# Two v loads issued from GpSimd's DMA queue instead of SyncE's, in a linear-attention and MLP kernel

## The chip, the cores and the metric

The kernel runs on one core of a Trainium2 chip. The metric is the device time of one execution in microseconds (us), as the median of several runs; the profiled execution is a further one, read by the hardware profiler.

A core has five engines that run side by side, each through its own list of instructions in order: TensorE (PE, with the weight loads as PEld), VectorE (DVE), ScalarE (ACT), GpSimd (POOL) and SyncE (SP). They wait for one another by semaphores. Loads from memory are DMAs, which an engine's queue issues and which the core's 16 DMA engines carry out.

## The reference

The first part is a gated linear attention with a state per head, over 4 batches, 8 heads, 768 positions and head size 48. The second is an MLP with the gate h * cos(h) on the 3072 tokens that result, each with 8 * 48 = 384 values.

```python
f = 1.0 / (1.0 + np.exp(-f_logit))
state = np.zeros((B, H, D, D))
for t in range(S):
    state = f[:, :, t, :, None] * state + np.einsum('bhd,bhe->bhde', k[:, :, t], v[:, :, t])
    y[:, :, t] = np.einsum('bhd,bhde->bhe', q[:, :, t], state)
x = y.transpose(0, 2, 1, 3).reshape(B * S, H * D)
h = x @ w_in                  # 384 -> 2048
out = (h * np.cos(h)) @ w_out # 2048 -> 384
```

## The kernel before

**Tiles.** The positions of a batch are taken 256 at a time; such a stretch, for all 8 heads, is a "pair" n, two neighbouring positions on each of the 128 partitions; there are 12 pairs, three for each batch. For a pair the kernel loads f, k, q and v, each as a tile of 128 partitions x 8 heads x 96 values in float32, 384 KB. Each head's 96 values on a partition are one contiguous run of 384 bytes in memory, so such a load has 1024 of these runs. For pairs 0 and 1 the loads of f, k and q are cut in two by heads (names f0.0, f0.1 and so on); v is not. The tiles come from pools of three buffers for each kind.

**Steps of a pair.** On ACT the logarithm of the gate is made from f (ex, ln, fx); TensorE sums it up along the positions (cum), ACT turns the sums into the decays eb and ei; qa and ka finish the factors of q and k, qm and km multiply them with the decays and write bf16 into the tile qk. For pairs 0 and 1, qm and km are given to POOL or VectorE one by one. TensorE turns q and k (tq, tk, line 435), VectorE or ACT copies the result from PSUM (qkt, line 197), TensorE makes the scores (sc, line 456), VectorE masks them (am, line 461). v is cast to bf16 in the tile vb (step vb, line 197), for pairs 0 and 1 by ACT, and four copies bring it in another order into vt. TensorE makes the state's increments from vb and qk (ps, line 479), VectorE carries the state (st, sz, lines 497 and 503), and TensorE makes the outputs (y, yi, line 531). The casts xe bring them to the MLP as x.

**The MLP.** It runs in units of 128 or 256 tokens: h (line 579) on TensorE, the cosine (co, line 584) on ACT, the product (g, line 561) on VectorE, and o (line 595) on TensorE. Its weights w0 and w1 are loaded and cast once (steps w and wc), beside the first pairs.

**Order.** The text ORDER writes out by hand, step by step, which engine does what, and in which order: the letter behind the colon is the engine (T TensorE, S ACT, V VectorE, G POOL, Y SyncE), the digits are buffer numbers. Each engine gets its steps in this order and does not overtake; a step waits on semaphores for what it reads and for the buffer that it writes. All loads stand on SyncE, except one half of f0 on ACT. Steps zf (line 264) are matmuls of zeros at the beginning that fill TensorE's time while there is no other work; their results aren't used.

The steps around the change, in the order of their engines: SyncE issues f0.1, k0.0, k0.1, f1.1, f1.0, q0.1, q0.0, then v0, f3, k1.1, k1.0, v1, f2, q1.0, q1.1, w0.1, w0.0. POOL has km0.0, qm0.0, a memset, ka1.0, ka1.1, km1.1. ACT has eb0.0, vb0, eb1.0, vt0.3, ei1.0, ex3 (of pair 3), eb1.1, ln3, ei1.1, vt0.0, vb1, ex2 (of pair 2). TensorE has ps0.1, ps0.0, tk0.1, tq0.0 after a group of zero matmuls.

The loads are issued by this function, whose second argument lists the engines that the plan may give the step to:

Of the kernel before, what the change touches and what calls it, by code (L numbers as in the profile page):

```python
# [15 lines left out]
B, H, S, D = 4, 8, 768, 48  # L16
# [13 lines left out]
SLOTS = {"f": 3, "k": 3, "q": 3, "v": 3, "sp": 3, "ls": 2, "b": 3, "bi": 3, "qk": 3, "vb": 3, "vt": 3, "qkt": 5, "am": 4,  # L30
         "sz": 4, "x": 4, "g": 5, "co": 4, "ot": 4}
WITHIN = 12
ZEROS = 54


ORDER = """
zvt.2:V zsp.1:V zsp.0:G zsz.3:V f0.1:Y0 f0.0:S zqk.0:G k0.0:Y0 ex0.1:S ex0.0:S k0.1:Y ln0.1:S1
zf0:T0 zf1:T0 zf2:T0 zf3:T0 zf4:T0 zf5:T0 zf6:T0 zf7:T0 zf8:T0 zf9:T0 cum0.1:T0 ln0.0:S cum0.0:T1
fx0.0:S ei0.1:S0 fx0.1:S ei0.0:S ka0.0:V f1.1:Y1 km0.0:G0 f1.0:Y ex1.1:S ka0.1:V zf10:T2 zf11:T2
zf12:T2 zf13:T2 zf14:T2 zf15:T2 zf16:T2 zf17:T2 tk0.0:T2 eb0.1:S0 ex1.0:S ln1.1:S1 ln1.0:S fx1.0:S  # L40
q0.1:Y0 q0.0:Y v0:Y0 fx1.1:S eb0.0:S qa0.1:V zqk.1:V qm0.1:V vb0:S0 f3:Y2 k1.1:Y1 km0.1:V qa0.0:V
zf18:T3 cum1.1:T3 zf19:T4 zf20:T4 zf21:T4 tq0.1:T0 cum1.0:T1 qm0.0:G zsz.2:G eb1.0:S1 vt0.3:S2
k1.0:Y ei1.0:S0 ex3:S zf22:T4 zf23:T4 zf24:T4 zf25:T4 zf26:T4 ps0.1:T4,5 ps0.0:T tk0.1:T v1:Y1 f2:Y0
qkt0.1:V0 eb1.1:S ln3:S0 ei1.1:S ka1.0:G q1.0:Y0 tq0.0:T ka1.1:G km1.1:G0 zvt.1:G vt0.0:S ad3:G1
vt0.1:G q1.1:Y vb1:S1 qkt0.0:V1 vt0.2:G zsz.1:G ex2:S w0.1:Y0 w0.0:Y1 k3:Y0 q3:Y1 w0.3:Y2 ln2:S1
vt1.2:S1 fy3:S zf27:T6 zf28:T6 zf29:T6 zf30:T6 zf31:T6 zf32:T6 sc0.0:T0 sz0.01:V2 sz0.00:V w0.2:Y3
# [142 lines left out]
def describe(nc, cpool, ppool, q, k, v, f_logit, moe_w_in, moe_w_out, out):  # L189
    G = Graph()  # L190
    eng = lambda e: {"DVE": nc.vector, "POOL": nc.gpsimd, "ACT": nc.scalar, "SP": nc.sync}[e]

    def tl(shape, dt, name):
        return cpool.tile(shape, dt, name=name)
# [4 lines left out]

    if ZEROS:  # L200
        zero = tl([128, 512], BF16, "zero")
# [57 lines left out]

    if ZEROS:  # L260
        for i in range(ZEROS):
            dump = Val(p1)
# [30 lines left out]

    def load(name, val, src, b, c, h0, h1):
        tok = src[b, h0:h1, 2 * C * c:2 * C * c + 2 * C, :] if nc is not None else None
        G.step(name, ("SP", "ACT") if name in ("f0.0", "f0.1") else ("SP",), lambda e: eng(e).dma_start(  # L296
            out=val.ap.rearrange("p h e d -> p h (e d)"),
            in_=tok.rearrange("h (p e) d -> p h (e d)", e=2)), writes=[val])

    def fetch(kind, pool, src, n, b, c, cut):  # L300

        whole = Val(pool)
        hs = [whole.part(lambda a, u=u: a[:, 4 * u:4 * u + 4]) for u in range(2)]
        if cut:
            for u in range(2):
                load(f"{kind}{n}.{u}", hs[u], src, b, c, 4 * u, 4 * u + 4)
        else:
            load(f"{kind}{n}", whole, src, b, c, 0, H)
        return whole, hs
# [335 lines left out]
def apart(tc, users, s, e, made):  # L645
# [14 lines left out]
    for t in {b // 2 for b in banks}:  # L660
# [5 lines left out]
        users[t].append((e, made, banks, uses))  # L666
        del users[t][:-WITHIN]

# [49 lines left out]
```

## Time and profile before

| | before |
|---|---|
| median of 3 runs | 183.03 us (183.0 to 183.31) |
| span of the profiled execution, first to last instruction | 180.9 us |
| runs' median less that span | 2.1 us |
| busy: PE, DVE, ACT, POOL | 172.6, 134.6, 130.7, 109.2 us |
| granted TensorE clock | 1.00 |
| SyncE's hardware queue q1 | 33.27 MB of 33.93 MB in all |

The profile is of one execution. It has no time of its own for that execution beyond its span, which runs from the first to the last of the program's instructions; what the runs have more lies before and behind these. An instruction's row has its start and duration, the engine and line, what it writes and reads, and in brackets how long the engine was idle before it and what ended that. Rows of SyncE (SPq) are issues: their duration is that of issuing, and the landing comes later. Rows of the same kind that follow one another are merged (x2), with their durations added.

### The profile page before, as it was taken

To read this page: it belongs to the slowest core of one execution; us is meant where nothing else is said; L and a number is where in the kernel's file an instruction comes from. 1 tells how busy PE (TensorE), PEld (TensorE's weight loads), DVE (VectorE), ACT (ScalarE), POOL (GpSimd) and SP (SyncE) were. 2 spreads that over 40 slices of the span, in tenths; PEclk is the share of its full clock that TensorE was granted. 3 is DMA by queue.
4 is the path that set the end of the run, shared out by engine and by line. 5 is a ranking of instruction groups with operands and counts; after the bars stand their busy time and mean duration, and the time that the engine had idled before them with its cause. 6 is when DMAs were issued, how large, how long until landed. Compare 5 with 4: busy or idle time off the path is not lost.

```text
span 180.9 us, 5814 instructions
## 1 busy us (share of the span) xinstructions
PE 172.6 (95%) x2460; PEld 123.9 (69%) x2464; DVE 134.6 (74%) x206; ACT 130.7 (72%) x187; POOL 109.2 (60%) x139
## 2 busy tenths in 40 slices
PE   7899789999999999999999999999999999999992
PEld 2455467785668977778667886658788767787651
DVE  5259988897595988897999697689888894356260
ACT  3985987777878899989997899769768452473221
POOL 4229899999969986989665977890798000000000
PEclk9999999999999999999999999999999999999999
DMA  5999999999999944986899999559927500110313
GB/s 149 261 261 276 343 320 341 250 318 284 301 265 233 274 83 123 252 210 145 122 180 308 173 267 278 124 131 251 203 92 182 100 4 0 43 47 4 130 43 131
DMA packets 72282, 33.93 MB, mean 188 GB/s; under 512 B 65344, under 2 KB 70720, under 8 KB 72256
## 3 DMA queue, kind: packets, MB, share of 16 engines
q1 hardware_dynamic: 71584, 33.27, 75.7%
q8 instruction: 19, 0.31, 0.7%
q10 hardware_dynamic: 672, 0.30, 0.6%
q14 instruction: 7, 0.06, 0.1%
HBM read 25.17 MB, written 4.72 MB: 165 GB/s over the span
## 4 chain that ended last, share of the span: by engine, by line
PE 81%; DMA 7%; ACT 3%; DVE 3%; SPq 2%; issue 1%; ACTq 0%
PE ps L595 35%; PE ps L579 33%; PE ps L531 5%; DMA f<-in_f_logit_dram 4%; PE ps L456 4%; DMA v<-in_v_dram 3%; SPq L296 2%; PE ps L479 2%; DVE g L561 1%; PE ps L435 1%; PE ps L374 1%; DVE am L461 1%; PE ps L264 1%; ACT f L344 0%; ACT f L329 0%
## 5 line engine op out<-in xcount | busy, mean ns | idle before, releaser
L561 DVE TENSOR_TENSOR g<-ps,co 128x1024 bf16<-128x1024 f32 x48 | 57.4, 1220 | 18.0 <-ACT co L584 16.7
L595 PE MATMUL ps<-w_out_bf,g 128*128 128x384 bf16 x384 | 68.9, 326 | 0.0
L579 PE MATMUL ps<-x,w_in_bf 128*128 128x256 bf16 (+1 forms) x624 | 68.1, 264 | 0.5 <-DVE x L197 0.4
L584 ACT ACTIVATE co<-ps,halfpi 128x1024 bf16<-128x1024 f32 x48 | 52.7, 1113 | 19.8 <-PE ps L579 19.5
L579 PEld LDWEIGHTS <-w_in_bf 128*128 128x128 bf16 x624 | 56.3, 98 | 9.2 <-DVE x L197 0.6
L595 PEld LDWEIGHTS <-g 128*128 128x128 bf16 x384 | 36.1, 98 | 21.4
L461 DVE TENSOR_TENSOR am<-ps,pmask 128x1024 bf16<-128x1024 f32 x24 | 28.7, 1218 | 5.2 <-PE ps L456 4.9
L404 POOL TENSOR_TENSOR qk<-k,bi 128x384 bf16<-128x384 f32 x22 | 22.0, 1008 | 5.4 <-ACT bi L391 4.7
L404 POOL TENSOR_TENSOR qk<-q,b 128x384 bf16<-128x384 f32 x21 | 20.8, 1000 | 2.7 <-DVE q L338 2.1
L197 POOL COPY vt<-vb 64x384 bf16<-64x384 bf16 x33 | 16.7, 507 | 1.6
L264 PE MATMUL ps<-zero 128*128 128x512 bf16 x50 | 14.6, 412 | 1.5 <-DVE zero L203 1.2
L503 DVE TENSOR_TENSOR sz<-ps,b 64x192 bf16<-64x192 f32 x40 | 14.1, 354 | 2.5 <-PE ps L479 1.6
L363 POOL TENSOR_TENSOR sp<-ls 128x384 bf16<-128x384 f32 x10 | 10.3, 1028 | 7.8 <-ACT ls L333 6.1
L341 POOL TENSOR_TENSOR q<-f,q 128x384 f32<-128x384 f32 x10 | 10.0, 998 | 8.0 <-DMA q<-in_q_dram 5.8
L329 ACT ACTIVATE f<-f 128x768 f32<-128x768 f32 (+1 forms) x14 | 10.4, 746 | 4.4 <-DMA f<-in_f_logit_dram 4.4
L497 DVE TENSOR_TENSOR ps<-ps,sz 64x192 f32<-64x192 f32 x32 | 11.7, 367 | 2.2 <-PE ps L479 1.1
L351 POOL TENSOR_TENSOR k<-k,f 128x384 f32<-128x384 f32 (+1 forms) x12 | 11.1, 931 | 3.4 <-DMA k<-in_k_dram 3.4
L197 ACT COPY ot<-ps 128x384 f32<-128x384 f32 (+1 forms) x14 | 6.1, 453 | 8.7 <-PE ps L595 8.7
L197 ACT CAST x<-ps 128x384 bf16<-128x384 f32 x12 | 5.5, 479 | 6.0 <-PE ps L531 6.0
L456 PE MATMUL ps<-qkt 48*64 48x128 bf16 (+1 forms) x304 | 8.7, 218 | 1.1 <-ACT x L197 0.8
L197 DVE CAST x<-ps 128x384 bf16<-128x384 f32 x12 | 6.4, 553 | 4.1 <-PE ps L531 3.9
L264 PEld LDWEIGHTS <-zero 128*128 128x128 bf16 x54 | 4.8, 103 | 5.9 <-issue 1.9
(64 smaller groups left out, 167.2 us busy)
## 6 DMA issues: line engine op xcount, KB each, us to landing
v<-in_v_dram SPq DMA_DIRECT2D x12, 384.0 KB, 5.9
out_dram<-ot SPq DMA_DIRECT2D x22, 192.0 KB, 2.3
f<-in_f_logit_dram SPq DMA_DIRECT2D x10, 384.0 KB, 6.0
k<-in_k_dram SPq DMA_DIRECT2D x10, 384.0 KB, 6.6
q<-in_q_dram SPq DMA_DIRECT2D x10, 384.0 KB, 6.7
g<-in_moe_w_in_dram SPq DMA_DIRECT2D x4, 768.0 KB, 7.5
g<-in_moe_w_out_dram SPq DMA_DIRECT2D x4, 768.0 KB, 6.1
k<-in_k_dram SPq DMA_DIRECT2D x4, 192.0 KB, 4.5
```

Of the source, the lines that this page charges most:

```text
L197: (nc.scalar.copy if e == "ACT" else eng(e).tensor_copy)(out=o, in_=i)
L264: G.step(f"zf{i}", ("PE",), lambda e, dump=dump: nc.tensor.matmul(dump.ap, lhsT=zero[:, 0:128], rhs=zero, start=True, stop=True), writes=[ ...
L351: eng(e).tensor_mul(out=w.ap[:, :, 0, :], in0=w.ap[:, :, 0, :], in1=t.ap[:, :, 0, :])
L404: G.step(f"{nm}{n}.{u}", ("POOL", "DVE") if cut else ("POOL",), lambda e, u=u, j=j, src=src, dec=dec: eng(e).tensor_mul(out=qkp[u][j].ap[: ...
L456: nc.tensor.matmul(o[t0:t1, r, 2 * a + g, :].rearrange("p (e n) -> p e n", e=2), lhsT=wide[s, t0 // 64, :] if turned else wide[s].rearrang ...
L461: G.step(f"am{n}.{u}", ("DVE",), lambda e, u=u, sc=sc: nc.vector.tensor_mul(out=am[u].ap.rearrange("p r b n -> p (r b) n"), in0=sc.ap.rear ...
L497: nc.vector.tensor_add(out=view()[s], in0=view()[s], in1=S0.ap[s, :, r, :])
L503: eng(e).tensor_mul(out=new.ap[s, :, r, :].rearrange("p (u a) n -> p u a n", u=2), in0=view()[s].rearrange("p (u a) n -> p u a n", u=2), i ...
L561: nc.vector.tensor_mul(out=o.rearrange("p b (n e) -> p b n e", e=2), in0=ph.ap.rearrange("p (b e n) -> p b n e", e=2, n=64), in1=co.ap.rea ...
L579: nc.tensor.matmul(ph.ap[:, i * T:(i + 1) * T].rearrange("p (g t) -> p g t", t=C), lhsT=w_in_bf[:, kk, f0:f0 + 128], rhs=xa[:, :, kk, :], ...
L584: G.step(f"co{m}.{j}", ("ACT",), lambda e, ph=ph, co=co: nc.scalar.activation(out=co.ap, in_=ph.ap, func=AF.Sin, bias=halfpi), reads=[ph], ...
L595: nc.tensor.matmul(po.ap[:, 0:DM], lhsT=gT.ap[:, j, i * C:(i + 1) * C], rhs=w_out_bf[:, j, :], start=(po.first and j == 4 * s), stop=(po.f ...
```

## The change

The loads v0 and v1 are issued by GpSimd instead of SyncE, and in the order they stand behind the product km0.0 on GpSimd, ahead of qm0.0. Nothing else moves: the other steps of every engine stay in their order, and the buffers are the same. The v loads of pairs 2 to 11 stay on SyncE.

```diff
+SWV = ("v0", "v1")
...
-fx0.0:S ei0.1:S0 fx0.1:S ei0.0:S ka0.0:V f1.1:Y1 km0.0:G0 f1.0:Y ex1.1:S ka0.1:V zf10:T2 zf11:T2
+fx0.0:S ei0.1:S0 fx0.1:S ei0.0:S ka0.0:V f1.1:Y1 km0.0:G0 v0:G0 v1:G1 f1.0:Y ex1.1:S ka0.1:V zf10:T2
...
-q0.1:Y0 q0.0:Y v0:Y0 fx1.1:S eb0.0:S qa0.1:V zqk.1:V qm0.1:V vb0:S0 f3:Y2 k1.1:Y1 km0.1:V qa0.0:V
+fx1.0:S q0.1:Y0 q0.0:Y fx1.1:S eb0.0:S qa0.1:V zqk.1:V qm0.1:V vb0:S0 f3:Y2 k1.1:Y1 km0.1:V qa0.0:V
...
-k1.0:Y ei1.0:S0 ex3:S zf22:T4 zf23:T4 zf24:T4 zf25:T4 zf26:T4 ps0.1:T4,5 ps0.0:T tk0.1:T v1:Y1 f2:Y0
+k1.0:Y ei1.0:S0 ex3:S zf22:T4 zf23:T4 zf24:T4 zf25:T4 zf26:T4 ps0.1:T4,5 ps0.0:T tk0.1:T f2:Y0
...
     def load(name, val, src, b, c, h0, h1):
...
-        G.step(name, ("SP", "ACT") if name in ("f0.0", "f0.1") else ("SP",), lambda e: eng(e).dma_start(
+        G.step(name, ("SP", "ACT") if name in ("f0.0", "f0.1") else ("POOL",) if name in SWV else ("SP",), lambda e: eng(e).dma_start(
```

More of the change, by code (lines that the diff above doesn't have):

```diff
@@ L38 @@
 zf0:T0 zf1:T0 zf2:T0 zf3:T0 zf4:T0 zf5:T0 zf6:T0 zf7:T0 zf8:T0 zf9:T0 cum0.1:T0 ln0.0:S cum0.0:T1
-fx0.0:S ei0.1:S0 fx0.1:S ei0.0:S ka0.0:V f1.1:Y1 km0.0:G0 f1.0:Y ex1.1:S ka0.1:V zf10:T2 zf11:T2
-zf12:T2 zf13:T2 zf14:T2 zf15:T2 zf16:T2 zf17:T2 tk0.0:T2 eb0.1:S0 ex1.0:S ln1.1:S1 ln1.0:S fx1.0:S
-q0.1:Y0 q0.0:Y v0:Y0 fx1.1:S eb0.0:S qa0.1:V zqk.1:V qm0.1:V vb0:S0 f3:Y2 k1.1:Y1 km0.1:V qa0.0:V
+fx0.0:S ei0.1:S0 fx0.1:S ei0.0:S ka0.0:V f1.1:Y1 km0.0:G0 v0:G0 v1:G1 f1.0:Y ex1.1:S ka0.1:V zf10:T2
+zf11:T2 zf12:T2 zf13:T2 zf14:T2 zf15:T2 zf16:T2 zf17:T2 tk0.0:T2 eb0.1:S0 ex1.0:S ln1.1:S1 ln1.0:S
+fx1.0:S q0.1:Y0 q0.0:Y fx1.1:S eb0.0:S qa0.1:V zqk.1:V qm0.1:V vb0:S0 f3:Y2 k1.1:Y1 km0.1:V qa0.0:V
 zf18:T3 cum1.1:T3 zf19:T4 zf20:T4 zf21:T4 tq0.1:T0 cum1.0:T1 qm0.0:G zsz.2:G eb1.0:S1 vt0.3:S2
-k1.0:Y ei1.0:S0 ex3:S zf22:T4 zf23:T4 zf24:T4 zf25:T4 zf26:T4 ps0.1:T4,5 ps0.0:T tk0.1:T v1:Y1 f2:Y0
+k1.0:Y ei1.0:S0 ex3:S zf22:T4 zf23:T4 zf24:T4 zf25:T4 zf26:T4 ps0.1:T4,5 ps0.0:T tk0.1:T f2:Y0
 qkt0.1:V0 eb1.1:S ln3:S0 ei1.1:S ka1.0:G q1.0:Y0 tq0.0:T ka1.1:G km1.1:G0 zvt.1:G vt0.0:S ad3:G1
```

## The prediction

> **What bounds the kernel now.** I read the page's busy shares and its chain first, then busy time by stretches, then the timelines of the five queues over the first 25 us, where the change lies.
>
> ```profile
> span 180.9 us, 5814 instructions
> PE 172.6 (95%) x2460; PEld 123.9 (69%) x2464; DVE 134.6 (74%) x206; ACT 130.7 (72%) x187; POOL 109.2 (60%) x139
> PE 81%; DMA 7%; ACT 3%; DVE 3%; SPq 2%; issue 1%; ACTq 0%
> ```
>
> TensorE sets the time, and the rest of the chain (DMA, ACT, DVE) has to lie where TensorE does not. The busy time by stretches says where (columns: stretch, its length, then busy time of PE, PEld, DVE, ACT, POOL with counts, granted clock, DMA share, GB/s):
>
> ```profile
> 0.70:1.75 1.05, 0.56 (x2) 0.28 (x3) 0.49 (x6) 0.51 (x1) 0.88 (x4) 1.00 0.00 0
> 2.75:3.75 1.00, 1.00 (x4) 0.33 (x3) 0.81 (x8) 0.00 (x0) 0.00 (x0) 1.00 1.12 308
> 5.00:9.00 4.00, 3.29 (x32) 1.90 (x32) 1.30 (x5) 3.97 (x12) 1.00 (x1) 1.00 1.27 262
> 9.00:15.00 6.00, 5.66 (x93) 3.17 (x94) 3.78 (x9) 5.05 (x13) 2.54 (x5) 1.00 1.28 263
> 12.36:24.52 12.16, 10.05 (x156) 5.17 (x158) 11.69 (x23) 10.10 (x21) 9.95 (x13) 1.00 1.15 301
> 36.00:176.00 140.00, 140.00 (x2022) 103.69 (x2021) 107.63 (x148) 102.93 (x136) 83.81 (x103) 1.00 0.71 167
> ```
>
> From 36 to 176 us TensorE is busy for 140.00 of 140.00 us at clock 1.00. So a delay of the useful work at the start reaches the end in full, unless slack ahead of 36 us swallows it. Before that, TensorE's busy time is partly the zero matmuls of line 264, which only fill. There the DMA queue runs at a steady 262 to 263 GB/s, and from 12.36 us VectorE is busy 11.69 of 12.16 us, that is, without room. What starts those two is what counts. From the chain in order of time, and the timelines of SP and ACT (start, duration, engine, line, what; in brackets the idle time before it and what ended it):
>
> ```profile
> 5.13 5.38 DMA v<-in_v_dram
> 10.51 7.11 DMA f<-in_f_logit_dram
> ```
> ```profile
> 0.73 0.46 SPq L296 DMA_DIRECT2D f<-in_f_logit_dram  x1
> 2.34 1.06 SPq L296 DMA_DIRECT2D f<-in_f_logit_dram  x2
> 5.13 0.69 SPq L296 DMA_DIRECT2D v<-in_v_dram  x1
> 5.86 1.36 SPq L296 DMA_DIRECT2D f<-in_f_logit_dram  x1
> 9.70 0.69 SPq L296 DMA_DIRECT2D v<-in_v_dram  x1
> 10.51 1.36 SPq L296 DMA_DIRECT2D f<-in_f_logit_dram  x1
> ```
> ```profile
> v<-in_v_dram SPq DMA_DIRECT2D x1, 384.0 KB, 5.5
> v<-in_v_dram SPq DMA_DIRECT2D x1, 384.0 KB, 5.4
> ```
> ```profile
> 10.67 0.83 ACT L197 CAST vb<-v 128x768 bf16<-128x768 f32 x1 [0.79 <-DMA v<-in_v_dram]
> 15.14 0.83 ACT L197 CAST vb<-v 128x768 bf16<-128x768 f32 x1 [0.23 <-DMA v<-in_v_dram]
> 17.71 0.84 ACT L329 ACTIVATE f<-f 128x768 f32<-128x768 f32 x1 [1.73 <-DMA f<-in_f_logit_dram]
> 23.06 0.46 ACT L197 CAST x<-ps 128x384 bf16<-128x384 f32 x1
> ```
>
> Both v loads are already waited for: v0, issued at 5.13, lands 5.5 later at 10.63 and ends an idle time of 0.79 on ACT; v1, issued at 9.70, lands at 15.1 and ends one of 0.23. What hangs on v0 is seen on TensorE and VectorE:
>
> ```profile
> 10.42 1.02 PE L264 MATMUL ps<-zero 128*128 128x512 bf16 x4
> 11.56 0.44 PE L479 MATMUL ps<-vb,qk 64*64 64x48 bf16 x32
> 11.93 0.62 PE L435 MATMUL ps<-ident,qk 128*128 128x128 bf16 x8
> 23.57 0.40 PE L456 MATMUL ps<-qkt 48*128 48x128 bf16 x8 [0.78 <-ACT x L197]
> ```
> ```profile
> 9.84 0.35 DVE L338 SCALAR_TENSOR_TENSOR q<-f,q 128x192 f32<-128x192 f32 x1
> 12.36 1.29 DVE L197 COPY qkt<-ps 128x1024 bf16<-128x1024 bf16 x2 [2.17 <-PE ps L435]
> 22.06 1.27 DVE L197 COPY qkt<-ps 128x1024 bf16<-128x1024 bf16 x2
> ```
>
> This is the path that decides. The cast vb0 ends at 10.67 + 0.83 = 11.50; at 11.56 TensorE runs ps0 (line 479), which reads vb; tk0.1 and tq0.0 (line 435) stand behind it in TensorE's order and run at 11.93; their result starts VectorE at 12.36 after 2.17 idle. VectorE then has no gap worth the name until the copies qkt1 of 22.06, which end at 23.33, and sc1.0 (line 456) follows at 23.57. The other path, f2's landing at 17.62 through ACT to the cast xe0.1 of 23.06, ends at that same matmul. So v0's path is only 23.57 - 23.33 = 0.24 us shorter than the one that the chain shows.
>
> **The change part by part.** *Off SP.* Two issues of 0.69 us go. SP's f3, k1.1 and k1.0 move up into v0's place, but f2 does not: its buffer is freed by qa0.0 on VectorE (9.84 + 0.35 = 10.19) and by ACT, and it is issued at 10.51 with or without the v loads ahead. The same bytes have to be through before f2 lands, unless the two queues together are faster; at 308 instead of 263 GB/s it would come up to 1 us earlier. I count that at nothing, because VectorE's path would still end where it does. The semaphore that a load shares with the eighth load before it is another one now; those loads landed long before.
>
> *Onto POOL.*
>
> ```profile
> 7.21 1.00 POOL L404 TENSOR_TENSOR qk<-k,bi 128x384 bf16<-128x384 f32 x1 [4.69 <-ACT bi L391]
> 10.32 1.00 POOL L404 TENSOR_TENSOR qk<-q,b 128x384 bf16<-128x384 f32 x1 [2.11 <-DVE q L338]
> 13.73 1.14 POOL L351 TENSOR_TENSOR k<-k,f 128x192 f32<-128x192 f32 x2 [2.06 <-DMA k<-in_k_dram]
> ```
>
> The loads stand behind km0.0, so v0 is issued at 7.21 + 1.00 = 8.21 instead of 5.13, 3.1 us later, and v1 right behind it. No POOL-issued load is in this trace. SP's issue of a half load (512 rows of 384 B) takes 0.46 to 0.53 when nothing holds it up, so I put POOL's writing of 1024 rows at 1.0 us. Both together take 2.0 of the 2.11 us in which POOL waits ahead of qm0.0: hidden, just. If each took 1.4, qm0.0 would start 0.7 late; that is covered again, because tq0.0 stands behind ps0, which waits for v0. A further 2.06 us of POOL idle time lies ahead of ka1.0.
>
> *When v0 lands.* Of SP's first load, issued at 0.73, no byte moves up to 1.75 (0 GB/s), 1.02 us at least; I take 1.05. So v0's first byte moves at 8.21 + 1.05 = 9.26 if POOL's rows are fetched as they are written, at 10.26 if only when all are; I take the middle, 9.76. From there the two queues share:
>
> ```profile
> q10 hardware_dynamic: 466, 0.17, 63.0%
> q1 hardware_dynamic: 367, 0.13, 49.4%
> ```
>
> That is 2.75:3.75, when ACT's queue (q10) and SP's (q1) both had loads of the same kind: 466 packets to 367, about one to one. The rate was 308 GB/s then; with SP alone it is 263. I take 285, so v0 gets 142, and its 393 KB need 2.76 us: it lands at 12.5, with 11.8 (9.26, 308) and 13.3 (10.26, 263) as ends. Against 10.63 that is 1.9 late (1.2 to 2.7).
>
> The Trainium skill, DMA: Bandwidth & Descriptors, section Issuing engines are not separate DMA queues, says that DMAs of all issuing engines run on the same 16 DMA engines and that several issuers save only issue time. By that rule there is no 308 and v0 would land 0.2 later than I take it, and the rows do not settle it, since a rate of 308 was seen only in the first microseconds. The same page, Latency and other measured facts, gives about 0.6 us to the first byte for SP's way and about 1 us for GpSimd's; the trace has at least 1.02 for SP, so I did not use its smaller figure.
>
> *What is queued behind the wait.* On ACT vb0 blocks eb1.0, vt0.3, ei1.0, ex3 and on to vb1 and ex2. ACT has 0.23 + 1.73 = 1.96 us of waiting left ahead of ex2, so a vb0 that is 1.9 late just fits, and ex2 still starts near 17.7. If v0 is later than 12.6, the surplus appears there too, alongside and not on top. On TensorE ps0 blocks tk0.1 and tq0.0, and through them VectorE starts 1.9 late at 14.3, with its 11.7 us of work still to do. k1.0 now shares its way with v0 and lands at about 14.2 instead of 13.7; km1.0, which needs it, runs on VectorE behind the delayed work, so it costs nothing more. v1 lands at about 12.5 + 2.76 = 15.3, ahead of the turn of vb1 on a late ACT.
>
> The sum: + 1.9 on VectorE's path, - 0.24 slack at 23.57, - 0 later, since nothing after 36 us has room: + 1.65 us. The profiled execution has 180.9 in its span and should have 182.6; the runs' median of 183.03 has 2.1 more around the span, which the change leaves. 183.03 + 1.65 = 184.7. The runs before spread by 0.31, so about 0.2% (0.37 us) is what can be told from no change.
>
> **Rivals.** *POOL's stream goes first.* If POOL's queue gets most of the DMA engines while it has rows, v0 needs 393 KB at 263 GB/s, 1.5 us, from 9.76: it lands at 11.3, 0.65 late, and the end moves by 0.4; with the late first byte (10.26) it is 0.9. About 183.7. Against it: two queues shared evenly in the one stretch that shows two. For it: those were two queues of one kind. It shows as f3 and k1.0 landing late while v0 and v1 land within 1.5 us of one another.
>
> *Writing the rows is slow.* The page's nearest price for POOL handling small items is its copy:
>
> ```profile
> L197 POOL COPY vt<-vb 64x384 bf16<-64x384 bf16 x33 | 16.7, 507 | 1.6
> ```
>
> 507 ns for 384 elements is 1.32 ns each; 1024 rows with a read and a write side are 2048 items or 2.7 us. If the bytes move only when all are written, v0 lands at 8.21 + 2.7 + 1.05 + 2.76 = 14.7, 4.1 late, which after the 0.24 costs 3.85: 186.9. qm0.0, behind 5.4 us of POOL time, would start at 13.6 and tq0.0 at about 14.7, late as well but not later than ps0. It decides from about 2 us per load.
>
> *Not slower.* POOL's first byte moves at 9.26, its stream goes first and the two queues run at 308 GB/s: 1.28 us, v0 lands at 10.5, before its old 10.63, and f2 lands up to 1 us earlier. Then VectorE starts 0.1 early, and the end is 182.9 to 183.0; with f2's path shortened as well, the gain can't exceed what VectorE's path gives. All three conditions are needed at once. It decides where v0 lands before 10.63 + 0.24 = 10.9. A real gain over 0.37 us would need a v0 before 10.3, 2.1 us after it is issued, which no 384 KB load here comes near (5.4 and 5.5), or a gain beyond 36 us that I don't see.
>
> That the change does not do what it says is hardly open: the loads are two instructions on GpSimd in place of two on SP, and the rest of each engine's order is the same.
>
> **How the numbers follow.** Forecast (even share, + 1.65, its own range 183.9 to 185.5): 0.50. POOL's stream first: 0.24, of which 0.04 falls within 0.2%. Slow writing: 0.16. Not slower: 0.10, of which 0.04 is faster by over 0.2%. So faster 0.04, same 0.10, slower 0.86. The range takes in the two neighbours: 183.3 to 187.0, with the slowest half of the slow case and most of the last outside.
>
> **What would show it.** In the changed profile: POOL issues at 8.2 and is back before or near 10.3; v0 lands at 11.8 to 13.3 and ACT waits 2 to 3 us for it ahead of vb0 instead of 0.79; VectorE's wait ahead of qkt0 grows from 2.17 to about 4; sc1.0 at 23.57 is late by 1.65 and is now released by VectorE, not by ACT; 36 us onwards is unchanged, only shifted. I am wrong if vb0 is not late, if its lateness does not reach sc1.0, if qm0.0 (POOL busy writing rows) is what VectorE waits for, or if TensorE, late at 36 us, makes the delay good afterwards.

## The result, and the profile after

| | before | changed | ratio, 95% interval |
|---|---|---|---|
| median of 4 runs each | 183.01 us (183.0 to 183.31) | 186.97 us (186.73 to 187.79) | 1.0231 [1.0202, 1.026] |
| span of the profiled execution | 180.9 us | 185.0 us | |

The change costs 3.96 us. The direction was forecast; the size was 1.65 us. In the kernels with a load from GpSimd the code has one line more, so L404 of before is L405 here.

From the page of the changed kernel: span, the two busiest engines' row, the queues, and the chain by engine.

```profile
span 185.0 us, 5816 instructions
PE 174.4 (94%) x2460; PEld 124.3 (67%) x2464; DVE 135.2 (73%) x206; ACT 130.8 (71%) x187; POOL 111.5 (60%) x141
q1 hardware_dynamic: 69504, 32.48, 71.0%
q0 software_dynamic: 224, 0.79, 1.7%
PE 82%; DMA 5%; DVE 4%; ACT 4%; POOL 3%; issue 1%; POOLq 0%; DVEq 0%
```

The two loads are now the 0.79 MB of a queue of their own, q0, in 224 packets: 3.5 KB each, where SyncE's q1 has 69504 packets for 32.48 MB, most of them one run of 384 bytes. The timelines of POOL, SP, ACT, TensorE and VectorE in the changed kernel (start, duration, engine, line, what; idle time before it and what ended that):

```profile
7.03 1.00 POOL L405 TENSOR_TENSOR qk<-k,bi 128x384 bf16<-128x384 f32 x1 [4.49 <-ACT bi L392]
7.97 1.94 POOL L297 DMA_DIRECT2D v<-in_v_dram  x2
10.16 0.99 POOL L405 TENSOR_TENSOR qk<-q,b 128x384 bf16<-128x384 f32 x1 [0.25 <-issue]
...
5.95 2.16 SPq L297 DMA_DIRECT2D k<-in_k_dram  x2
10.10 0.37 SPq L297 DMA_DIRECT2D f<-in_f_logit_dram  x1
...
13.51 0.83 ACT L198 CAST vb<-v 128x768 bf16<-128x768 f32 x1 [3.80 <-DMA v<-in_v_dram]
...
14.40 0.44 PE L480 MATMUL ps<-vb,qk 64*64 64x48 bf16 x32 [3.12 <-ACT vb L198]
...
15.20 1.29 DVE L198 COPY qkt<-ps 128x1024 bf16<-128x1024 bf16 x2 [5.18 <-PE ps L436]
17.17 0.54 DVE L405 TENSOR_TENSOR qk<-k,bi 128x384 bf16<-128x384 f32 x1
21.90 0.87 DVE L339 SCALAR_TENSOR_TENSOR q<-f,q 128x192 f32<-128x192 f32 x1
```

POOL does what was forecast: it issues at 7.97, writes for 1.94 us, and qm0.0 starts at 10.16, 0.16 earlier than before. But v0 lands at 13.49, 2.84 us later than before, so ACT waits 3.80 us in place of 0.79, TensorE has a hole of 3.12 us ahead of ps0, and VectorE starts at 15.20 in place of 12.36.

The landings, in the order of landing (us):

| | q0.0 | v0 | f3 | k1.1 | k1.0 | v1 | f2 |
|---|---|---|---|---|---|---|---|
| before | 9.14 | 10.65 | 12.16 | 12.91 | 13.66 | 15.12 | 17.62 |
| changed | 8.97 | 13.49 | 10.48 | 11.24 | 12.00 | 15.00 | 16.51 |

Each row is one line of transfers: 1.5 us after the one ahead for a whole load of 384 KB, 0.75 for a half, whichever queue it came from. (Before's f2 is the exception; there a fetch of instructions took one DMA engine for about 1.2 us at 13.95.) v0 has fallen back by f3, k1.1 and k1.0, which is 1.5 + 0.75 + 0.75 = 3.0 us. What moved in single microseconds of the changed kernel, by queue (packets, MB, share of 16 engines; first 11 to 12 us, then 12 to 13):

```profile
q0 software_dynamic: 60, 0.24, 96.7%
q1 hardware_dynamic: 32, 0.01, 5.7%
...
q0 software_dynamic: 82, 0.28, 110.0%
```

There is no even sharing: f2, issued on SP at 10.10, gets almost nothing while q0 has rows. f2's rows were written behind v1's, though, so this kernel alone does not tell whether POOL's queue goes first or whatever was written first (see v1 alone and v0 alone below). The busy time by stretches in the changed kernel (stretch, length, busy time of PE, PEld, DVE, ACT, POOL, granted clock, DMA share, GB/s):

```profile
15.00:16.00 1.00, 1.00 (x10) 0.57 (x8) 0.80 (x2) 0.98 (x3) 0.00 (x0) 0.80 1.29 261
16.00:17.00 1.00, 1.00 (x3) 0.30 (x2) 0.95 (x3) 1.00 (x3) 0.00 (x0) 0.50 1.34 286
17.00:18.00 1.00, 0.64 (x9) 0.34 (x8) 0.71 (x2) 1.00 (x4) 0.49 (x1) 0.50 1.01 342
18.00:19.00 1.00, 1.00 (x6) 0.13 (x2) 0.80 (x1) 1.00 (x2) 1.00 (x3) 0.50 1.04 379
40.06:180.06 140.00, 140.00 (x2022) 103.71 (x2021) 107.62 (x148) 103.02 (x136) 82.23 (x102) 1.00 0.68 162
```

After the hole TensorE is granted half the clock, from about 15.6 to 19.0 us. The last row is the stretch of before's 36 to 176, shifted by 4.06: 140.00 of 140.00 us busy, the same 2022 matmuls. The loss is complete by then, and next to nothing of it is made good.

### The profile page after: what moved, and what is told of

The parts are those of the page before. It is cut to its first block, busy times and chain, and to the rows that moved or that the text cites. A ratio compares the mean times of both kernels' runs of the same rounds, so it can differ in the third digit from the quotient of the medians.

```text
span 185.0 us, 5816 instructions
## 1 busy us (share of the span) xinstructions
PE 174.4 (94%) x2460; PEld 124.3 (67%) x2464; DVE 135.2 (73%) x206; ACT 130.8 (71%) x187; POOL 111.5 (60%) x141
## 3 DMA queue, kind: packets, MB, share of 16 engines
q1 hardware_dynamic: 69504, 32.48, 71.0%
## 4 chain that ended last, share of the span: by engine, by line
PE 82%; DMA 5%; DVE 4%; ACT 4%; POOL 3%; issue 1%; POOLq 0%; DVEq 0%
PE ps L596 35%; PE ps L580 33%; PE ps L532 5%; PE ps L457 4%; DMA v<-in_v_dram 3%; POOL qk L405 2%; PE ps L480 2%; DMA f<-in_f_logit_dram 2%; PE ps L265 1%; PE ps L436 1%; ACT f L330 1%; DVE qk L405 1%; PE ps L375 1%; DVE ps L498 1%; POOL w_in_bf L198 1%
## 5 line engine op out<-in xcount | busy, mean ns | idle before, releaser
L405 POOL TENSOR_TENSOR qk<-k,bi 128x384 bf16<-128x384 f32 x22 | 21.9, 1004 | 9.4 <-ACT bi L392 8.8
L405 POOL TENSOR_TENSOR qk<-q,b 128x384 bf16<-128x384 f32 x21 | 20.8, 1001 | 0.8 <-issue 0.2
L198 POOL COPY vt<-vb 64x384 bf16<-64x384 bf16 x33 | 17.2, 524 | 1.6
L265 PE MATMUL ps<-zero 128*128 128x512 bf16 x50 | 16.5, 455 | 1.5 <-DVE zero L204 1.2
L498 DVE TENSOR_TENSOR ps<-ps,sz 64x192 f32<-64x192 f32 x32 | 11.7, 366 | 2.2 <-PE ps L480 1.1
```

Source lines behind the costliest of these rows:

```text
L198: (nc.scalar.copy if e == "ACT" else eng(e).tensor_copy)(out=o, in_=i)
L265: G.step(f"zf{i}", ("PE",), lambda e, dump=dump: nc.tensor.matmul(dump.ap, lhsT=zero[:, 0:128], rhs=zero, start=True, stop=True), writes=[ ...
L405: G.step(f"{nm}{n}.{u}", ("POOL", "DVE") if cut else ("POOL",), lambda e, u=u, j=j, src=src, dec=dec: eng(e).tensor_mul(out=qkp[u][j].ap[: ...
L498: nc.vector.tensor_add(out=view()[s], in0=view()[s], in1=S0.ap[s, :, r, :])
```

## The experiments

**One queue, another place.** Everything stays on SyncE; v0 and v1 are only put behind k1.0.

```diff
-q0.1:Y0 q0.0:Y v0:Y0 fx1.1:S eb0.0:S qa0.1:V zqk.1:V qm0.1:V vb0:S0 f3:Y2 k1.1:Y1 km0.1:V qa0.0:V
+q0.1:Y0 q0.0:Y f3:Y2 k1.1:Y1 k1.0:Y v0:Y0 v1:Y1 fx1.1:S eb0.0:S qa0.1:V zqk.1:V qm0.1:V vb0:S0 km0.1:V qa0.0:V
```

> Both v loads on SyncE again, but behind f3, k1.1 and k1.0, so that nothing is on GpSimd and only the place in the line is that of the changed kernel. Theory O (all loads are served in the order of their issue, whichever queue issues them; v0 is late by the bytes of f3, k1.1 and k1.0, 1.5 + 0.75 + 0.75 us): v0 lands at about 13.6 us and the time is that of the changed kernel, 186.5 to 187.3. Theory L (a load that GpSimd issues starts late by itself, some 2.6 us after its issue) says nothing against a late v0 here, but then part of the 3.96 us is GpSimd's own (1.94 us of writing, the vector work beside it), and this kernel should be faster than the changed one by over 0.5 us: 185.5 to 186.3.

Measured: 186.83 us (186.66 to 187.13), ratio 1.021 [1.0188, 1.0233], the changed kernel's time without GpSimd's queue. On the timeline of ACT:

```profile
13.53 0.83 ACT L197 CAST vb<-v 128x768 bf16<-128x768 f32 x1 [3.81 <-DMA v<-in_v_dram]
```

v0 lands at 13.51, within 0.02 of the changed kernel. So the place in the line by itself makes v0 late and gives a loss of this size. That the two times agree to 0.14 is in part chance: h0.01 is 3.74 late here and 3.66 in the changed kernel, which then loses 0.4 more at g0.0 (below), so that at 40 us it is 3.75 against 4.06; by the mask of pair 8 (am8.0) it is 4.02 against 3.96.

**v0 one place later only**, on SyncE, behind f3:

```diff
-q0.1:Y0 q0.0:Y v0:Y0 fx1.1:S eb0.0:S qa0.1:V zqk.1:V qm0.1:V vb0:S0 f3:Y2 k1.1:Y1 km0.1:V qa0.0:V
+q0.1:Y0 q0.0:Y f3:Y2 v0:Y0 fx1.1:S eb0.0:S qa0.1:V zqk.1:V qm0.1:V vb0:S0 k1.1:Y1 km0.1:V qa0.0:V
```

> Both v loads on SyncE, v0 behind f3 alone: half the displacement. Theory O: v0 lands at 10.65 + 1.5 = 12.15, VectorE's first qkt copy starts at 13.9, and less the 0.24 us of slack at sc1.0 the end is 1.26 us later: 184.3. TensorE's gap ahead of ps0 is about 1.5 us; if a gap of that length already lowers the clock, up to 0.9 more: 185.2. The prediction's slack is wrong if the end moves by 1.5 or more at a clock of 1.00.

Measured: 185.2 us (185.01 to 185.37), ratio 1.0116 [1.0097, 1.0134]. v0 lands 1.54 late, at 12.19, with the clock at 1.00 throughout, yet the end is 2.2 later. More is lost than v0 is late, so something else adds to it.

**The clock.** The changed kernel with 14 products of zeros in TensorE's hole, ahead of ps0.1:

```diff
-ZEROS = 54
+ZEROS = 68
...
-... zf26:T4 ps0.1:T4,5 ps0.0:T tk0.1:T f2:Y0
+... zf26:T4 zf54:T4 zf55:T4 ... zf67:T4 ps0.1:T4,5 ps0.0:T tk0.1:T f2:Y0
```

> The changed kernel with 14 more matmuls of zeros on TensorE right ahead of ps0.1, about 3.0 us at 0.215 each, in the gap in which it waits 3.12 us for vb0. Theory C (of the 3.96 us some 0.9 come from the granted TensorE clock, which fell to 0.50 from about 15.6 to 19.0 us after that gap, so that the zero matmuls and sc0.0 behind tq0.0 were late): the clock stays at 1.00, sc0.0 starts at about 16.6 instead of 17.54, and the time falls by 0.5 to 0.9 us, to 186.0 to 186.5. Theory P (the rest beyond v0's 3.0 us comes from VectorE, whose instructions of two SBUF operands take up to twice as long beside GpSimd's shifted work): the clock stays up, but the time stays within 0.2 us of 186.97.

Measured: 187.75 us (187.44 to 188.31), ratio 1.0259 [1.0233, 1.0284]; no gain. The clock stayed at 1.00 (columns as above):

```profile
16.00:17.00 1.00, 1.00 (x12) 0.44 (x11) 0.95 (x3) 1.00 (x4) 0.00 (x0) 1.00 1.28 271
```

sc0.0 started 1.0 us earlier than in the changed kernel, but at qkt1.0 0.12 of it was left. Later, at 127 us, the DMA that turns q of pair 9 landed 1.36 us later than in the changed kernel and cost 0.5 at sc9.1.

**Where the extra goes.** VectorE's product qm1.1 and POOL's cast wc0.1 beside it, on the timelines of before, of the changed kernel and of v0 behind f3:

```profile
21.19 0.56 DVE L404 TENSOR_TENSOR qk<-q,b 128x384 bf16<-128x384 f32 x1
...
22.18 2.87 POOL L197 CAST w_in_bf<-g 128x1536 bf16<-128x1536 f32 x2
```
```profile
25.06 1.14 DVE L405 TENSOR_TENSOR qk<-q,b 128x384 bf16<-128x384 f32 x1
...
24.32 3.20 POOL L198 CAST w_in_bf<-g 128x1536 bf16<-128x1536 f32 x2
```
```profile
21.44 0.54 DVE L404 TENSOR_TENSOR qk<-q,b 128x384 bf16<-128x384 f32 x1
23.15 1.70 DVE L404 TENSOR_TENSOR qk<-q,b 128x384 bf16<-128x384 f32 x1
...
22.97 3.20 POOL L197 CAST w_in_bf<-g 128x1536 bf16<-128x1536 f32 x2
```

The first of the two casts, wc0.1, takes 1.46 to 1.47 us, so it ends at 23.64, 25.79 and 24.43. Before, qm1.1 is through when it starts. In the other two qm1.1 meets it and ends 0.41 and 0.42 after the cast's end, whenever it started. So VectorE's product waits out POOL's whole cast. To test it, qm1.1 was put directly behind qm1.0 on VectorE in four kernels:

```diff
-... qa1.1:V qm1.0:V wc0.2:G ... st1.00:V st1.01:V qm1.1:V v2:Y1
+... qa1.1:V qm1.0:V qm1.1:V wc0.2:G ... st1.00:V st1.01:V v2:Y1
```

*v0 behind f3, with this move:*

> The kernel in which SyncE issues v of pair 0 behind f3, with one step moved on VectorE: the product qm1.1 directly behind qm1.0, ahead of sz0.10, st1.00 and st1.01. C, the collision: there qm1.1 ran from 23.15 to 24.85, 1.70 us where it takes 0.56 in the kernel before, because GpSimd's cast wc0.1 (22.97 to 24.43) ran beside it. Moved, it starts at about 21.95 and is over at about 22.5, ahead of the cast; sz1.00 then starts at about 23.7 instead of 24.88, and the run takes 183.9 to 184.5 us, against 185.2 without the move. R, the stretch is a wait for something else, an input or a free buffer: qm1.1 then ends near 24.8 wherever it starts, holds the three steps behind it, and the run takes 185.2 to 186.3.

Measured: 183.98 us (183.82 to 184.06), ratio 1.0057 [1.0044, 1.0069]: 1.2 faster than without the move, as the clash asks. Timelines of VectorE and POOL in it:

```profile
20.29 1.16 DVE L338 SCALAR_TENSOR_TENSOR q<-f,q 128x192 f32<-128x192 f32 x1
21.38 1.01 DVE L404 TENSOR_TENSOR qk<-q,b 128x384 bf16<-128x384 f32 x2
...
20.21 1.03 POOL L363 TENSOR_TENSOR sp<-ls 128x384 bf16<-128x384 f32 x1
21.18 2.13 POOL L197 COPY vt<-vb 64x384 bf16<-64x384 bf16 x2
```

qm1.0 and qm1.1 take 1.01 us together. Now POOL waits: its two copies take 2.13 us where two took 1.06 just before. And qa1.1 (20.29), which takes 0.34 in the kernel before, has met POOL's sum (20.21 to 21.24).

*The changed kernel with the move:*

> The changed kernel with the same move of qm1.1 directly behind qm1.0. C: there qm1.1 ran 1.14 us, 25.06 to 26.20, beside the cast wc0.1, 24.32 to 25.79. Moved, it starts at about 23.86 and is nearly through when the cast starts, so sz1.00 starts 0.5 to 0.6 earlier and the run takes 186.3 to 186.6 us, against 186.97. If it still touches the cast's start and is stretched by it, the run stays at 186.9 to 187.5. R: 187.0 to 188.0.

Measured: 186.9 us (186.5 to 187.49), ratio 1.022 [1.0198, 1.0241], not to be told from 186.97. The clash only moved: qm1.0 and qm1.1 together took 1.63 us there, beside POOL's copies, and qkt1.0 started 0.04 earlier.

*The changed kernel with the zeros and the move:*

> The changed kernel with fourteen products of zeros in TensorE's gap, which kept the granted clock at 1.00, and the same move of qm1.1. With the zeros alone sc0.0 was 1.0 us earlier than in the changed kernel, but qm1.1 then waited out the cast (24.38 to 26.07) and the run won nothing. C: qm1.1 moved runs at about 23.2 to 23.7, sz1.00 at about 24.9 instead of 26.10, and the run takes 186.0 to 186.9 us against 187.75 with the zeros alone; at 30 us the pipeline is then 0.6 to 0.8 earlier than that of the changed kernel with the same move, and that is what the lower clock costs. R: no better than 187.6.

Measured: 186.05 us (185.92 to 186.36), ratio 1.0176 [1.0161, 1.0191]: 1.7 faster than with the zeros alone (1.1 of it at qkt1.0; that DMA at 127 us gives 0.24 more, the rest stays open), and 0.85 faster than with the move alone. At h0.01 of the profiled executions it is 1.16 ahead of the latter. So holding the clock is worth 0.85 us of the run once qm1.1 does not wait for the cast.

*The kernel before with the move:*

> The kernel before with the same move of qm1.1. C: in the kernel before qm1.1 (21.19 to 21.75) is over 0.43 us ahead of the cast wc0.1 (22.18) and loses nothing, so the move wins nothing: 182.8 to 183.3 us. The move by itself is thus not what makes the other three faster. R: 183.0 to 183.9.

Measured: 183.05 us (182.66 to 184.32), ratio 1.0019 [1.0, 1.0039]; no gain. Timelines of VectorE and POOL:

```profile
19.73 1.82 DVE L404 TENSOR_TENSOR qk<-q,b 128x384 bf16<-128x384 f32 x2
...
19.84 1.30 POOL L363 TENSOR_TENSOR sp<-ls 128x384 bf16<-128x384 f32 x1 [0.92 <-ACT ls L333]
```

Here the move puts qm1.1 into the way of another POOL step: it ends at 21.55, 0.41 after that step's end (21.14), and qkt1.0 is 1.01 late. So the expectation that nothing is lost was wrong for the instruction and right for the time: of the 1.01 only 0.27 is left at h0.01, behind room of about 0.8 (below), and f2, which landed 0.27 later here than in before, would leave as much by itself.

**Only one of the two loads on GpSimd.** v1 alone:

```diff
-SWV = ("v0", "v1")
+SWV = ("v1",)
```

> Only v1 on GpSimd behind km0.0, v0 back on SyncE in its old place. Theory O: v0 lands at 10.6 as before; v1 is issued at 8.0 to 9.0, ahead of k1.0, which SyncE issues at about 8.9, so v1 lands at about 14.4 (ahead of its old 15.1) and k1.0 at about 15.1 instead of 13.7; ka1.0 and km1.0 wait for that, and the time rises by about 1.2 us, to 184.2. Theory S (queues share evenly): v1 at about 14 to 15 and k1.0 at 14.2 to 14.5, 0.5 to 0.8 later: 183.5 to 183.8. Theory L: v1's bytes start 2.6 us after its issue at the earliest, which the line ahead of it hides; it says the same as O for v1, and k1.0 not later than 13.7 if its bytes are then ahead: 183.0.

Measured: 186.09 us (185.73 to 186.2), ratio 1.0161 [1.0141, 1.0181]. v0 is on time (10.55), but v1, written from 8.05 on, gets ahead of k1.0, issued on SP at 8.91: k1.0 lands at 15.09, and km1.0 is 1.42 late. What moved by queue from 12 to 13 us, over 3 us after k1.0's issue:

```profile
q0 software_dynamic: 63, 0.25, 100.3%
q1 hardware_dynamic: 24, 0.01, 4.1%
```

Here SP had a load waiting, and POOL's went first. qa1.1 (1.15 us) and qm1.1 (1.70 us) then meet POOL. Theory O had both landings right; its time, 184.2, lacks these two clashes and the 0.4 at g0.0 (below). A load that comes too early can cost nearly as much as one that comes late.

v0 alone, with v1 on SyncE behind k1.0:

> Only v0 on GpSimd, v1 on SyncE behind k1.0. Theory O: v0 is issued at about 8.0 behind f3, k1.1 and k1.0 and lands at 13.5, v1 (SyncE, at about 8.2) at about 15.0, so it is the changed kernel's time, 186.97 within 0.4 us. If a part of the loss is v1's or the second 0.9 us of GpSimd's writing, it is faster by that part.

Measured: 188.69 us (188.63 to 189.25), ratio 1.0324 [1.0301, 1.0348], the slowest with an interval. v0 was issued by POOL at 7.94 and v1 by SP at 8.09, but v1's rows went first. From 11 to 12 us:

```profile
q1 hardware_dynamic: 682, 0.26, 127.3%
q0 software_dynamic: 1, 0.00, 1.6%
```

v0 landed at 14.95, now with v1's bytes ahead of it too. So POOL's queue does not go first as such. This kernel, v1 alone and the changed one all fit a line ordered by when a load's rows have been written, not by when its instruction starts: here SP was through with v1's at 8.78, and POOL, which needs about 1 us, with v0's at 8.99. Why POOL's and SP's loads are not shared evenly, no run shows.

**Nothing ahead of v0.** The changed kernel with f3, k1.1 and k1.0 moved behind f2:

> The changed kernel with f3, k1.1 and k1.0 (and the step ex3 that reads f3) moved behind f2, so that SyncE has nothing waiting when GpSimd issues v0 at about 8.0; the last load ahead, q0.0, lands at 9.0. Read for v0's landing, not for its time (k1 is late here, so it is slower). Theory O: v0's bytes start at 9.0 to 9.5 and it lands at 10.5 to 11.2, v1 at 12.0 to 12.7. Theory L: v0's bytes start no earlier than 10.5, 2.6 us after the issue, the DMA engines stand idle from 9.0 to 10.5, and v0 lands at 12.0 or later.

Measured, in a single run: 190.62 us; the late k1.0 (19.44) explains the time. The line was empty, and of q0's bytes 0.04 MB moved between 9 and 10 us, which at 262 GB/s puts the first at about 9.85, 1.8 us after the issue at 8.06. v0 landed at 12.65.

**Another queue.** v0 and v1 from ACT's queue, behind ex1.0:

> v0 and v1 issued from ACT's queue, behind ex1.0, at about 8.0 us, the moment at which GpSimd issues them in the changed kernel; SyncE as there. Theory O: v0 lands at about 13.5 and v1 at 15.0, as from GpSimd, and the time is within 0.6 us of 186.97 (ACT has 3.8 us of waiting there for its issues). Theory S (two queues of the hardware kind share one to one, the prediction's term): v0 lands at 12.0 to 12.6 and k1.0 at about 14, and the time is about 185.5. Theory L: v0 lands ahead of 13, since it is not GpSimd that issues it.

Measured, in a single run: 186.82 us; v0 landed at 13.69, v1 at 14.98. What moved by queue (q10 is ACT's) from 11 to 12 us, then 12 to 13:

```profile
q10 hardware_dynamic: 365, 0.14, 70.2%
q1 hardware_dynamic: 315, 0.12, 58.6%
...
q10 hardware_dynamic: 521, 0.19, 95.0%
q1 hardware_dynamic: 190, 0.07, 33.1%
```

ACT's queue does share with SP's: k1.0 landed at 13.70 with v0, in place of 12.00. With POOL's it did not. v0 is late all the same.

**Earlier on GpSimd.** v0 and v1 ahead of km0.0, right behind zqk.0:

```diff
-... zqk.0:G k0.0:Y0 ... km0.0:G0 v0:G0 v1:G1 f1.0:Y
+... zqk.0:G v0:G0 v1:G1 k0.0:Y0 ... km0.0:G0 f1.0:Y
```

> v0 and v1 from GpSimd as in the changed kernel, but ahead of km0.0, behind the memset of qk, so issued at 2.6 and 3.6 us. Read for the landings. Theory O: v0 lands among f1 and q0, at about 8 to 9.2, v1 at about 10 to 10.7, and q0.0, which SyncE issues at 4.3, at about 12 instead of 9.0; qa0.0 and qm0.0 are late by 3 us, and the time is 185 to 186.5. Theory S: v0 and v1 share with SyncE's loads from 4.5 on; v0 lands at about 8.5, v1 at about 11, q0.0 at about 11.5. Theory L: v0's bytes start at 5.2, the same as O within what can be told.

Measured, in a single run: 186.83 us. v0 landed at 8.87 and v1 at 11.16, but q0.0 at 11.91 in place of 9.14, and k1.0 at 14.79; qa1.0 was 3.27 late. The line has no free place in this stretch: whoever is moved forward pushes another load back.

**0.41 us at g0.0.** In the changed kernel VectorE's gate product g0.0 starts 0.49 after its input co0.0 ends; in before it is 0.09. All eight kernels with v0 or v1 on GpSimd show 0.49 or 0.50, the others 0.09 or 0.10. Two variants of the kernel before: v of pair 3, which is issued after g0.0, from GpSimd's queue, and w0.0 exchanged with k3 on SyncE.

```diff
-qkt3.0:V0 v3:Y0
+qkt3.0:V0 v3:G0
```

> The kernel before, with nothing moved at the start: only v of pair 3, issued at 37.3, after g0.0, goes through GpSimd's queue. In the changed kernel the gate product g0.0 on VectorE starts 0.49 us after its input co0.0 ends, in the kernels without a load from GpSimd 0.09 us after. P, a load from GpSimd anywhere in the program brings the 0.41 us: the gap here is 0.5. Q, it comes with the queue being used ahead of g0.0: 0.09. W, it comes with which of the eight completion counters the load of w0.0 uses, which g0.0 waits for (number 7 in the changed kernel, 1 before and here): 0.09. The run as a whole: 182.9 to 184.5 us under all three.

Measured, in a single run: 182.7 us, gap 0.10.

```diff
-w0.0:Y1 k3:Y0
+k3:Y0 w0.0:Y1
```

> The kernel before with the loads w0.0 and k3 exchanged in SyncE's order, which moves w0.0 to the next completion counter (2 in place of 1); no load from GpSimd. W: g0.0 starts about 0.5 us after co0.0's end in place of 0.09, or after h1.00, whichever it is that the counter stands for. P and Q: 0.09. The run: 182.8 to 184.0 us.

Measured, in a single run: 183.5 us, gap 0.10. A load from GpSimd somewhere in the program does not bring it, nor does that other completion counter. By the semaphores in the traces, w0.0 has counter 0 in the kernels with v1 alone and v0 alone on GpSimd, not 7, and the gap of 0.50 is there as well, so it is not counter 7 as such. It goes with loads from that queue ahead of g0.0; why, stays open.

No kernel here beat the one before by more than the spread of its own runs (182.64 to 183.34 us).

## Why the prediction was right in direction and wrong in size

At 40 us the changed kernel is 4.06 behind (o2.0). The starts of the steps on the way, against before, give the sum; each later term is the difference between two neighbouring steps:

| term | us | from |
|---|---|---|
| v0's cast vb0 starts late | +2.84 | 13.51 against 10.67 |
| km1.0 doesn't meet POOL any more (0.54 in place of 0.93) | -0.4 | the lateness of qa1.0 with the zeros (2.35) against vb0's (2.77) |
| half clock after TensorE's hole | +1.1 | qa1.0 is 3.51 late |
| qa1.0 meets POOL (0.87 in place of 0.52) | +0.36 | qm1.0 is 3.87 late |
| qm1.1 waits out wc0.1 | +0.58 | qkt1.0 is 4.45 late |
| room on TensorE ahead of h0.01 | -0.79 | h0.01 is 3.66 late |
| g0.0, open | +0.4 | 4.06 late, and so to the end within 0.1 |

The rows of before for the second and the fourth term:

```profile
14.36 0.93 DVE L404 TENSOR_TENSOR qk<-k,bi 128x384 bf16<-128x384 f32 x1
18.39 0.52 DVE L338 SCALAR_TENSOR_TENSOR q<-f,q 128x192 f32<-128x192 f32 x1
```

The split between the second and third row is worked out by the kernel with the zeros, where the clock held; that the clock's 1.1 was not won back there is since qa1.1 and qm1.1 then waited for POOL instead (1.16 and 1.70 us). So the clock and the clash are not additive: what comes earlier meets POOL earlier. The same terms add up for v0 behind f3 (qa1.0 +1.13, qa1.1's clash to +1.96, qm1.1's to +3.10, room to +2.31) and with the move (+1.07, +1.90, +1.85, +1.06).

*Onto POOL*: right. 7.97 for 8.21, 1.94 us of writing for 2.0, hidden as forecast; slow writing, and a late qm0.0, are out. That the slow-writing rival's 186.9 is the figure nearest to the measured 186.97 is luck, since its step did not happen. *Off SP*: right in that nothing is won there.

*When v0 lands*: this step failed, 12.5 for 13.49. The first byte was taken at 9.76, and with nothing ahead it was about 9.85. But the step left out two things that the trace of before already held. First, the bytes that SP had queued: in the changed kernel f3, k1.1 and k1.0 were through at 10.74 only, by adding up what moved. Second, the landing: adding up the same way in before, the loads from q0.0 to k1.0 landed 1.18 us after their bytes were through, and v1 1.13. Those two add 2.2 us; that v0 then got the line to itself, 1.5 us in place of the 2.76 of an even share, gave 1.3 back. A test on before would have shown it: by the prediction's own formula SP's v0, issued at 5.13, would land at 5.13 + 1.05 + 1.5 = 7.7, and it landed at 10.65. A load in a full line is priced by its place, not by its issue.

*Even sharing* was read from two queues of one kind. ACT's queue did share with SP's, POOL's did not. The rival that POOL's stream goes first had v0 and v1 1.5 us apart right (1.51), but its other sign did not come, since f3 and k1.0 landed early (10.48 and 12.00 for 12.16 and 13.66), and with v0 alone on POOL it was SP's load that went first. Its time (183.7) was too low for the same missing line.

The Trainium skill, DMA: Bandwidth & Descriptors, section Issuing engines are not separate DMA queues, says that several issuers save only issue time; the trace agrees, 1.5 us per 384 KB with either queue. The same page, section Queues, rings and completion order, has each DMA engine take turns between queues by whole packets. With POOL's packets nine times SP's (3.5 KB to 384 bytes), that would by an estimate leave SP a tenth. With v1 alone on POOL it was 0.01 of 0.26 MB, less than that, and with v0 alone POOL had one packet of 683; the measurements decide.

*The slack* of 0.24 was too small: it was 0.78 or 0.79 in every kernel whose qkt1.0 is over 1.8 us late. The row for it was quoted, the 0.78 us that TensorE waits for ACT at 23.57. The prediction took the end of the merged row of two copies, 23.33, but sc1.0 reads only the first of them, qkt1.0, which is through at 22.73.

*What is queued behind the wait* failed too, and this is the larger miss. The step that failed is VectorE starting late "with its 11.7 us of work still to do": a VectorE step was taken to last as long later as before, and TensorE as having no memory of a hole, so the sum has no term for either. From qkt0.1 to qkt1.0 it was 9.70 us in before (12.36 to 22.06) and 11.30 in the changed kernel (15.20 to 26.50), and g0.0 took 0.4 more, so 2.0 us stand where the forecast had nothing.

The Trainium skill, SBUF — State Buffer, section SBUF: two separate sides, says that a VectorE operation with two inputs in SBUF and a GpSimd operation that reads SBUF lock each other out for the whole instruction; the trace agrees, in both directions (qm1.1 1.70 us for 0.56, two POOL copies 2.13 for 1.06). The Trainium skill, TensorE: Matmul & The Clock Gate, Part 1, has TensorE fall to half clock after an idle window of about 3.4 us, which it must be busy through again to get it back. Here holes of 3.12 us (the changed kernel), 2.86 (v0 behind k1.0 on SyncE) and 2.69 (ACT's queue) were enough, so the measurements decide and less than the page's figure will do; behind one of 1.62 (v0 behind f3) the clock stayed at 1.00. The 0.50 lasted about 3.4 us in the first.

The forecast's 1.65 was thus 1.9 - 0.24 where the runs have 2.84 - 0.79 = 2.05 for those two terms, and 2.0 for what is in the other rows: of the 2.4 us that were missing, 0.4 is v0's landing and the slack together, and 2.0 is what was put at nothing.

## What to carry to other kernels

Where the transfers form one full line, moving a load to another queue moves its place in that line: count the bytes issued ahead of it, check the formula on a load of the trace at hand, and add the lag from last byte to landing. A delay on one engine also shifts its work against that of a neighbour: look for pairs of operations (here VectorE's products of two SBUF tiles and POOL's casts) that stand just clear of each other, and price what happens when they meet. Holes of 2.7 to 3.1 us on TensorE cost once more here, by the clock.

## What the runs showed of the hardware

- From the moment at which, by adding up, a load's bytes were through to its landing: 1.13 to 1.18 us for SP's loads in before, 1.2 to 1.3 for POOL's in the changed kernel.
- POOL wrote the rows of two 384 KB loads (1024 runs of 384 bytes each) in 1.94 us; with nothing ahead, the first byte moved about 1.8 us after the issue.
- While POOL's queue moved 0.24 to 0.28 MB per us, SP's moved 0.01 or nothing, in v1 alone with k1.0 issued over 3 us earlier; in v0 alone SP's moved 0.26 and POOL's one packet. ACT's and SP's queues shared (0.14 and 0.12).
- A VectorE product of two SBUF tiles that met a POOL operation (qm1.1, 0.54 to 0.56 us alone) ended 0.41 or 0.42 us after that operation's end, in the changed kernel, v0 behind f3, the zeros and the kernel before with the move.
- The granted clock fell to 0.50 behind TensorE holes of 3.12, 2.86 and 2.69 us, and not behind one of 1.62.
